# Attention and spectral mixing on one core: an earlier fold, a reordered end and equal output steps

## The chip, the core and the metric

The kernel runs on one core of a Trainium2 chip. Five engines work side by side, each through its own list of instructions in the order in which the program issued them: TensorE (PE, with its weight loads shown apart as PEld), VectorE (DVE), ScalarE (ACT), GpSimd (POOL) and SyncE (SP). POOL issues the transfers of the weights, SP those of the output. Engines wait for each other and for transfers through semaphores. The metric is the time of one execution in microseconds on the device; lower is better.

## The reference

First a causal attention with a forgetting gate, for 8 batches, 8 heads, 576 positions and 64 columns per head:

```python
scores = scale * np.matmul(q, k.transpose(0, 1, 3, 2))
cum = np.cumsum(np.log(np.clip(f, 0.0001, 1.0)), axis=-1)
scores = np.where(causal, -1e9, scores + cum[..., :, None] - cum[..., None, :])
attn = softmax(scores); x = np.matmul(attn, v)        # then heads side by side: (8, 576, 512)
```

Then a mixing in the frequency domain over the positions: the lowest 64 modes of x are multiplied, each by its own complex 512 x 512 matrix, brought back to positions and added, and a gated product ends it:

```python
X = np.fft.rfft(x, axis=1)
Yr = np.einsum('bmd,mde->bme', Xr, w_r) - np.einsum('bmd,mde->bme', Xi, w_i)
Yi = np.einsum('bmd,mde->bme', Xr, w_i) + np.einsum('bmd,mde->bme', Xi, w_r)
u = x + np.fft.irfft(Y, n=S, axis=1)
out = u + np.maximum(u @ w_ch, 0.0)
```

The weights w_r and w_i are 64 x 512 x 512 float32 each, 134 MB together, and are read once. The output is 9.44 MB of float32.

## The kernel before

There are three stages. The order on every engine is the order in which the source issues the work.

**Attention** runs over 32 pairs of heads and leaves x in `x_all` (128 positions per block; a batch has five blocks, the last with 64 positions only). Beside it the first weight tiles are loaded and multiplied.

**The weights' stage.** Modes are handled in groups of four, u = 0 to 15, and the 512 input columns in four quarters dc = 0 to 3. A weight tile (u, dc) has 1 MB in SBUF (2 MB in memory, cast to bfloat16 on the way). A pool of seven such buffers and POOL's transfers, issued one ahead of the next in the order of `wseq`, form a stream. For u < 15 `spec_mms` (L194) multiplies into an accumulator A; then `Yb` on DVE (L744) and four small products `yps` (L747) turn the result into mode columns: `YT` for the first 12 groups (96 rows of modes, real and imaginary), `YL` for the last four (32 rows). The last group, u = 15, is done with the weights as the stationary operand (`spec_cols`, L211: 32 products of 16 columns for one quarter), its sum over quarters being held in `accT`. The last tile (15,3) comes in four transfers, one for each mode.

In the gaps of this stage the PE does two other things for each batch. `xw(b)` computes x times w_ch into `XW[b]`. `fold(b)` adds the first 96 rows of modes, brought back to positions: `fold_modes` makes `y_sb` and `yw_sb` (the modes, and the modes times w_ch), then for each block three products and two copies put x + y back into `x_all` and XW + yw back into `XW`. Batches 0 to 5 are folded in u = 12 to 14, batch 6 in front of (15,1), batch 7 around (15,2).

**The output stage.** What is missing is the last 32 rows of modes. For a step the PE puts the *base* into PSUM (x_all or XW times an identity, L785) and adds the *rest* (32 rows of last modes times the inverse basis, L800) for two quantities, U and Z. ACT copies U (L854), DVE forms max(Z, 0) + U into `o_sb` (L855), and SP sends it (L860, L865). `last_modes(h)` makes the last modes for four batches: `pyl` turns them, `pywl` multiplies them by w_ch, and `yl` receives both.

The steps go over pairs of batches p and blocks sb: 16 steps of two 128-row tiles (512 KB), and 4 steps of one tile in which the two 64-row blocks of the pair lie one above the other (two transfers of 128 KB). The beginning of the stage in source order is

```python
first = bases(0)
AT = psU.tile([128, NEB, 8, B], F32, tag="u", name="AT2")
spec_cols(AT, NEB - 1)
...
last_modes(0)
for i, (p, sb) in enumerate(blocks):
    if i == 7:
        last_modes(1)
    U, Z = first if i == 0 else bases(i)
    rest(i, U, Z)
```

so the bases of step 0 are issued ahead of the products of the last weight tile. U and Z have four PSUM banks each (`psU`, `psZ`), taken over from the pools of the stage before.

Of the kernel before, what the change touches and what calls it, by code (L numbers as in the profile page):

```python
# [10 lines left out]
F32 = mybir.dt.float32  # L11
BF16 = mybir.dt.bfloat16
I32 = mybir.dt.int32
ALU = mybir.AluOpType
# [9 lines left out]
def kernel(  # L24
# [11 lines left out]
    nc = tc.nc  # L36
    B, H, S, Dh = q.shape
    NM = moe_w_r.shape[0]
    D = H * Dh
    assert S == 576 and Dh == 64 and D == 512 and H == 8, (B, H, S, Dh)  # L40
    assert NM == 64 and B == 8
    NSB = 5
# [5 lines left out]
    NF = 12  # L48
# [149 lines left out]
    def spec_cols(AT, dc):  # L198
        u = NU - 1
        w8 = wtile.pop((u, dc))  # L200
        for j in range(4):
            for eb in range(NEB):
                for n in range(2):
                    m = 4 * u + j
                    if dc < 2:
                        c0 = m * 24 + (8 if n == 0 else 0)
                        lhsT, rhs = w8[:, n, j, eb * 128 : (eb + 1) * 128], XS[:, dc, c0 : c0 + 16]
                    else:
                        c0 = 24 * n + (8 if dc == 2 else 0)
                        lhsT, rhs = w8[:, j, n, eb * 128 : (eb + 1) * 128], XPv[:, c0 : c0 + 16, m]  # L210
                    nc.tensor.matmul(  # L211
                        AT[:, eb, 2 * j : 2 * j + 2, :].rearrange("p c b -> p (c b)"),
                        lhsT=lhsT,
                        rhs=rhs,
                        start=(n == 0),
                        stop=(n == 1),
                    )
# [405 lines left out]
    with ExitStack() as bctx:  # L623
# [7 lines left out]

        with ExitStack() as mctx:
# [6 lines left out]
            def xw(b):  # L639

                xT = xtp.tile([128, NEB, S], BF16, tag="xT", name="xT")
                for eb in range(NEB):
                    ptr = psT.tile([128, S], BF16, tag="t", name="ptr")
                    for sc in range(NSB):
                        ns = SBLK[sc]
                        nc.tensor.transpose(
                            ptr[:, sc * 128 : sc * 128 + ns],
                            x_all[:ns, eb, b, sc, :],
                            ident_bf[:ns, :ns],
                        )  # L650
                    nc.vector.tensor_copy(xT[:, eb, :], ptr[:, :])  # L651
                if b < 3:
                    XW[b] = xw2.tile([128, NSB, D], BF16, tag="xw", name="XW")
                else:
                    XW[b] = yx[:, b - 3, :].bitcast(BF16).rearrange("p (s e) -> p s e", s=NSB)
                for sb in range(NSB):
                    Ms = SBLK[sb]
                    pxw = psX.tile([128, D], F32, tag="x", name="pxw")
                    for eb in range(NEB):
                        nc.tensor.matmul(  # L660
                            pxw[:Ms, :],
                            lhsT=xT[:, eb, sb * 128 : sb * 128 + Ms],
                            rhs=wch[:, eb, :],
                            start=(eb == 0),
                            stop=(eb == NEB - 1),
                        )
                    nc.scalar.copy(XW[b][:Ms, sb, :], pxw[:Ms, :])  # L667
# [27 lines left out]
            def fold(b, ys, sbs):  # L695

                y_sb, yw_sb = ys
                for sb in sbs:
                    Ms = SBLK[sb]
                    bi = BI[:KF, sb * 128 : sb * 128 + Ms]  # L700
                    pu = psX.tile([128, D], F32, tag="x", name="pu")
                    nc.tensor.matmul(
                        pu[:Ms, :], lhsT=ident_bf[:Ms, :Ms], rhs=x_all[:Ms, :, b, sb, :], start=True, stop=False
                    )
                    nc.tensor.matmul(pu[:Ms, :], lhsT=bi, rhs=y_sb[:KF, :], start=False, stop=True)  # L705
                    nc.scalar.copy(  # L706
                        x_all[:Ms, :, b, sb, :], pu[:Ms, :].rearrange("p (g c) -> p g c", g=NEB)
                    )
                    pz = psX.tile([128, D], F32, tag="x", name="pz")
                    nc.tensor.matmul(pz[:Ms, :], lhsT=bi, rhs=yw_sb[:KF, :], start=True, stop=True)  # L710
                    nc.vector.tensor_tensor(
                        XW[b][:Ms, sb, :], pz[:Ms, :], XW[b][:Ms, sb, :], ALU.add
                    )

            xw_plan = {2: 0, 3: 1, 5: 2, 6: 3, 7: 4, 8: 5, 9: 6, 10: 7}
            for u in range(NU):
# [4 lines left out]
                for dc in range(first, NEB - 1 if last else NEB):  # L721
                    if dc == NEB - 1 and u in xw_plan:
                        xw(xw_plan[u])
                    split = NSB
                    if u >= NF and dc < 3:
                        b = 2 * (u - NF) + dc - 1
                        split = 2 if b == B - 1 else NSB
                        ys = fold_modes(b)
                        fold(b, ys, range(split))
                    if last:  # L730
                        AT = psA.tile([128, NEB, 8, B], F32, tag="a", name="AT1")
                        spec_cols(AT, dc)
                        nc.vector.tensor_tensor(
                            accT[:], AT[:].rearrange("p e c b -> p e b c"), accT[:], ALU.add
                        )
# [3 lines left out]
                    if split < NSB:  # L739
                        fold(b, ys, range(split, NSB))  # L740
# [22 lines left out]
        usb = bctx.enter_context(tc.tile_pool(name="usb", bufs=4))  # L763
        psU = bctx.enter_context(tc.tile_pool(name="psU", bufs=4, space=PSUM))
        psZ = bctx.enter_context(tc.tile_pool(name="psZ", bufs=4, space=PSUM))
        blocks = [(p, sb) for p in range(B // 2) for sb in range(NSB)]
        yl = {}

        def parts(n):

            p, sb = blocks[n]
            Ms = SBLK[sb]
            if sb < NSB - 1:
                return [(2 * p + k, k, slice(0, Ms), sb, Ms) for k in range(2)]
            return [(2 * p + k, 0, slice(Ms * k, Ms * k + Ms), sb, Ms) for k in range(2)]

        def bases(n):

            pts = parts(n)
            nt = 1 + pts[1][1]  # L780
            U = [psU.tile([128, D], F32, tag="u", name="U") for _ in range(nt)]
            Z = [psZ.tile([128, D], F32, tag="z", name="Z") for _ in range(nt)]
            for which, ps in enumerate((U, Z)):
                for b, k, rows, sb, Ms in pts:
                    nc.tensor.matmul(  # L785
                        ps[k][rows, :],
                        lhsT=ident_bf[:Ms, :Ms],
                        rhs=XW[b][:Ms, sb, :] if which else x_all[:Ms, :, b, sb, :],
                        start=True,
                        stop=False,  # L790
                    )
            return U, Z

        def rest(n, U, Z):

            for which, ps in enumerate((U, Z)):
                for b, k, rows, sb, Ms in parts(n):
                    r = (b + 2 * which) % 4
                    grp = slice(32 * r, 32 * r + 32)
                    nc.tensor.matmul(  # L800
                        ps[k][rows, :],
                        lhsT=BI4[grp, sb * 128 : sb * 128 + Ms],
                        rhs=yl[b // 4][which][grp, :],
                        start=False,
                        stop=True,
                    )

        def last_modes(h):

            py = psU.tile([128, D], F32, tag="u", name="pyl")  # L810
            for eb in range(NEB):
                nc.tensor.matmul(
                    py[:, eb * 128 : (eb + 1) * 128],
                    lhsT=YL[:, eb, 4 * h : 4 * h + 4, :].rearrange("p b c -> p (b c)"),
# [5 lines left out]
            for eb in range(NEB):  # L820
                for n in range(2):
                    b = 4 * h + 2 * (1 - n)
                    nc.tensor.matmul(
                        pyw[64 * n : 64 * n + 64, :],
                        lhsT=YL[:, eb, b : b + 2, :].rearrange("p b c -> p (b c)"),
                        rhs=wch[:, eb, :],
                        start=(eb == 0),
                        stop=(eb == NEB - 1),
                    )
            yl[h] = [ylpool.tile([128, D], BF16, tag="yl", name="yl") for _ in range(2)]  # L830
            nc.scalar.copy(yl[h][0][:], py[:])
            nc.vector.tensor_copy(yl[h][1][:], pyw[:])

        first = bases(0)
        AT = psU.tile([128, NEB, 8, B], F32, tag="u", name="AT2")
        spec_cols(AT, NEB - 1)
        for h in range(2):
            bs = slice(4 * h, 4 * h + 4)
            nc.vector.tensor_tensor(
                YL[:, :, bs, KL - 8 : KL],  # L840
                AT[:, :, :, bs].rearrange("p e c b -> p e b c"),
                accT[:, :, bs, :],
                ALU.add,
            )
        last_modes(0)
        for i, (p, sb) in enumerate(blocks):
            if i == 7:
                last_modes(1)
            U, Z = first if i == 0 else bases(i)
            rest(i, U, Z)  # L850
            o_sb = wpool.tile([128, 2, D], F32, tag="w8", name="o_sb")
            for n in range(len(U)):
# [5 lines left out]
            s0 = sb * 128  # L858
            if len(U) == 2:
# [3 lines left out]
            else:  # L863
                for b, k, rows, _, Ms in parts(i):
                    nc.sync.dma_start(out[b, s0 : s0 + Ms, :], o_sb[rows, 0, :])  # L865
# [30 lines left out]
```

## Time and profile before

| what | value |
|---|---|
| median of 3 runs | 441.06 us (440.43 to 441.65) |
| the profiled execution | 442.7 us |
| its span, first to last instruction | 440.7 us |
| busy: PE, DVE, ACT, POOL | 344.5, 268.4, 233.3, 129.7 us |
| read from HBM, written | 163.73 MB, 9.44 MB |
| mean granted clock of the PE | 0.936 |
| last `AT` product issued from | 405.03 us |
| first output transfer issued | 410.50 us |
| last tile of `o_sb` done | 435.36 us |

Span and profiled execution differ by 2.0 us, which lie around the instructions. All times below are counted from the start of the span. Busy time says little on its own here, because the three stages have different limits; the chain of waits and the timeline of the last 60 us say what sets the end.

### The profile page before, as it was taken

Reading aid. Unit: us, or ns where it says so; the run is one execution under the profiler, and the core shown is the slowest. Engines: PE = TensorE matmul, PEld = TensorE weight load, DVE = VectorE, ACT = ScalarE, POOL = GpSimd, SP = SyncE. Lnnn points to the kernel's source line nnn. Section 1 sums busy time; section 2 is a strip of 40 time slices with the busy share of each in tenths; the row PEclk is TensorE's granted clock in tenths of the full one; section 3 lists DMA queues with packets and bytes.
Section 4 is the critical chain, followed back from the end, with each engine's and each line's share of the span. In section 5 each row is a group of like instructions: output and inputs, shape, how many; then the busy total and the mean of one; then the engine's idle time right before and its main releaser. Section 6 shows DMA issues by size and latency. Waiting matters only on the chain.

```text
span 440.7 us, 10287 instructions
## 1 busy us (share of the span) xinstructions
PE 344.5 (78%) x4295; PEld 189.9 (43%) x4305; DVE 268.4 (61%) x641; ACT 233.3 (53%) x355; POOL 129.7 (29%) x199
## 2 busy tenths in 40 slices
PE   1678878889889889898893694797885788979993
PEld 0455555555555565555551241343442233325331
DVE  6678888777887778888871221223231356635885
ACT  4567678778787665665640031132222355734673
POOL 6544444453454444444222111012211221100000
PEclk9999999999999999999997598599989699969997
DMA  8999999999999999999999999999999999992698
GB/s 190 205 234 221 230 220 231 232 228 227 231 231 222 231 222 229 221 230 224 232 212 212 212 212 212 212 212 212 211 212 210 211 210 210 210 210 53 219 347 294
DMA packets 68349, 96.75 MB, mean 220 GB/s; under 512 B 3536, under 2 KB 45008, under 8 KB 68304
## 3 DMA queue, kind: packets, MB, share of 16 engines
q0 software_dynamic: 62800, 85.64, 104.9%
q1 hardware_dynamic: 5504, 10.47, 6.8%
q8 instruction: 33, 0.54, 0.4%
q14 instruction: 12, 0.10, 0.1%
HBM read 163.73 MB, written 9.44 MB: 393 GB/s over the span
## 4 chain that ended last, share of the span: by engine, by line
DMA 39%; PE 34%; DVE 19%; ACT 3%; issue 3%; POOL 1%; DVEq 0%; POOLq 0%; ACTq 0%
DMA w<-in_moe_w_i_dram 22%; DMA w<-in_moe_w_r_dram 15%; DVE vT L384 5%; DVE x_all L492 4%; DVE qkT L360 4%; PE pav L477 4%; PE A L194 4%; PE sps L432 3%; PE tv L382 3%; PE pd L521 3%; PE vp L393 2%; PE U L785 2%; DMA qk<-in_k_dram 2%; PE Z L785 2%; DVE vn L372 2%
## 5 line engine op out<-in xcount | busy, mean ns | idle before, releaser
L439 ACT ACTIVATE et<-sps 128x1024 bf16<-128x1024 f32 x96 | 96.0, 1050 | 12.6 <-PE sps L432 10.2
L744 DVE TENSOR_TENSOR Yb<-A,yx 128x512 bf16<-128x512 f32 x15 | 10.4, 692 | 67.6 <-PE A L194 67.6
L477 PE MATMUL pav<-vs,et 128*128 128x65 bf16 (+1 forms) x896 | 51.2, 197 | 0.2 <-DVE vn L372 0.2
L360 DVE COPY qkT<-tp 128x640 bf16<-128x640 bf16 x64 | 48.8, 763 | 3.1 <-PE tp L355 3.0
L477 PEld LDWEIGHTS <-et 128*128 128x128 bf16 (+1 forms) x896 | 36.5, 102 | 17.2 <-issue 13.3
L194 PE MATMUL A<-w,XP 128*16 128x512 bf16 (+1 forms) x240 | 22.6, 457 | 27.1 <-DMA w<-in_moe_w_i_dram 15.6
L660 PE MATMUL pxw<-wch,xT 128*128 128x512 bf16 (+1 forms) x152 | 39.1, 403 | 1.0 <-DVE xT L651 0.4
L432 PE MATMUL sps<-qkT 64*128 64x512 bf16 (+4 forms) x320 | 38.9, 306 | 1.1 <-DVE qkT L360 1.1
L492 DVE TENSOR_TENSOR x_all<-pav,rcp 128x384 bf16<-128x384 f32 (+2 forms) x96 | 36.2, 377 | 3.3
L355 PE MATMUL tp<-ident_bf,qk 128*64 128x128 bf16 x576 | 29.3, 231 | 9.9 <-DMA qk<-in_k_dram 9.9
L384 DVE COPY vT<-tv 128x576 bf16<-128x576 bf16 x32 | 24.2, 757 | 19.3 <-PE tv L382 19.3
L667 ACT CAST XW<-pxw 128x512 bf16<-128x512 f32 (+1 forms) x15 | 8.8, 585 | 48.3 <-PE pxw L660 48.3
L165 POOL DMA_DIRECT2D w<-in_moe_w_r_dram x16 | 11.9, 743 | 70.1 <-PE A L194 56.7
L404 ACT COPY vs<-vp 128x576 bf16<-128x576 bf16 x32 | 20.5, 640 | 21.4 <-PE vp L400 21.4
L156 POOL DMA_DIRECT2D w<-in_moe_w_r_dram x27 | 20.5, 759 | 38.5 <-PE A L194 8.6
L667 ACT CAST yx<-pxw 128x512 bf16<-128x512 f32 (+1 forms) x25 | 14.6, 585 | 32.4 <-PE pxw L660 32.4
L165 POOL DMA_DIRECT2D w<-in_moe_w_i_dram x19 | 13.3, 700 | 55.8 <-PE A L194 26.1
L109 POOL DMA_DIRECT2D qk<-in_q_dram x32 | 19.7, 614 | 33.8 <-PE tp L355 7.8
L706 ACT CAST x_all<-pu 128x512 bf16<-128x512 f32 (+1 forms) x40 | 23.4, 584 | 9.0 <-PE pu L705 8.0
L491 DVE RECIPROCAL rcp<-pav 128x6 f32<-128x6 f32 (+2 forms) x96 | 16.2, 169 | 16.3 <-PE pav L477 16.1
L156 POOL DMA_DIRECT2D w<-in_moe_w_i_dram x27 | 20.4, 756 | 17.5 <-DMA w<-in_moe_w_i_dram 8.2
L109 POOL DMA_DIRECT2D qk<-in_k_dram x32 | 19.4, 605 | 20.2 <-DMA w<-in_moe_w_r_dram 6.5
(134 smaller groups left out, 666.5 us busy)
## 6 DMA issues: line engine op xcount, KB each, us to landing
w<-in_moe_w_r_dram POOLq DMA_DIRECT2D x16, 1024.0 KB, 29.6
w<-in_moe_w_i_dram POOLq DMA_DIRECT2D x15, 1024.0 KB, 32.1
w<-in_moe_w_r_dram POOLq DMA_DIRECT2D x27, 512.0 KB, 11.1
w<-in_moe_w_i_dram POOLq DMA_DIRECT2D x27, 512.0 KB, 12.5
vt<-in_v_dram POOLq DMA_DIRECT2D x29, 288.0 KB, 10.6
out_dram<-o_sb SPq DMA_DIRECT2D x16, 512.0 KB, 3.4
qk<-in_q_dram POOLq DMA_DIRECT2D x32, 144.0 KB, 10.7
qk<-in_k_dram POOLq DMA_DIRECT2D x32, 144.0 KB, 10.8
```

Of the source, the lines that this page charges most:

```text
L109: nc.gpsimd.dma_start(qk[64 * n : 64 * n + 64, :, :], src[b, 2 * g : 2 * g + 2, :, :].rearrange("h (p r) d -> p h (r d)", p=64),)
L156: nc.gpsimd.dma_start(w8[:, t, :, :], src[4 * u : 4 * u + 4, dc * 128 : (dc + 1) * 128, :].rearrange("m p e -> p m e"),)
L165: nc.gpsimd.dma_start(w8[:, j : j + step, :, :].rearrange("p m r e -> p m (r e)"), src[m : m + step, 256:512, :].rearrange("m (p r) e -> p ...
L194: nc.tensor.matmul(A[32 * j : 32 * j + M, :], lhsT=lhsT, rhs=rhs, start=st_, stop=sp_)
L355: nc.tensor.transpose(tp[64 * hp : 64 * hp + 64, r - r0, :, :].rearrange("p n c -> p (n c)"), qk[:, hp, r * 64 : r * 64 + 64], ident_bf[:, :],
L360: nc.vector.tensor_copy(st[i]["T"][:].rearrange("p n (c r) -> p n c r", r=9)[:, :, :, r0:r1], tp[:, 0 : r1 - r0, :, :].rearrange("p r n c ...
L384: nc.vector.tensor_copy(st[i]["vT"][:].rearrange("p (c r) -> p c r", r=9), tv[:].rearrange("p r c -> p c r"))
L432: nc.tensor.matmul(ps[:, hp, c : c + n], lhsT=KT[sl, jb * 128 : jb * 128 + 128], rhs=QT[sl, i0 : i0 + n], start=True, stop=True,)
L439: nc.scalar.activation(st[i]["et"][:, T, :, :], ps[:], ACT.Exp, scale=scale)
L477: nc.tensor.matmul(pav[:Ms, sb % 3, hp, :], lhsT=eblk(i, hp, jb, sb), rhs=rhs, start=(jb == 0), stop=(jb == sb),)
L492: nc.vector.tensor_tensor(x_all[:ns, g, b, lo:hi, :].rearrange("p s (h d) -> p s h d", h=2), pav[:ns, lo % 3 : lo % 3 + n, :, 0:Dh], _stri ...
L660: nc.tensor.matmul(pxw[:Ms, :], lhsT=xT[:, eb, sb * 128 : sb * 128 + Ms], rhs=wch[:, eb, :], start=(eb == 0), stop=(eb == NEB - 1),)
```

## The change

Five edits, all behind the last of the u = 14 products of quarter 2, apart from one that only moves data:

1. The 64-row blocks of an odd batch are kept in rows 64 to 127 of the even batch's tile (`place`), in `x_all` and in `XW`, from `xw` and `fold` on.
2. Folding is laid out by a table `before`: batch 6's modes and first two blocks stand ahead of the products of (14,3), its other blocks ahead of (15,1); batch 7's modes and two blocks stand ahead of (15,2); its other three blocks each ahead of one mode of (15,3).
3. (15,3) is multiplied inside the weights' loop, mode by mode, and so ahead of the output's bases.
4. In `last_modes`, `pywl` is four products with 128 columns of weights in place of eight with 64. Its halves come out in the other order and are copied crosswise: DVE copies 64 rows, and ACT the other 64 rows after the first step's copies.
5. The output has 18 steps of two tiles: 16 as before, and 2 that join the 64-row blocks of two pairs of batches (as steps 7 and 16). A base of such a tile is one full product. Steps 0, 1 and 17 send each tile by itself. Output transfers: 24 before, 23 now.

```diff
+        def place(b, sb):
+            if sb < NSB - 1:
+                return slice(0, 128), b
+            return slice(64 * (b % 2), 64 * (b % 2) + 64), b - b % 2
...
-                    nc.scalar.copy(XW[b][:Ms, sb, :], pxw[:Ms, :])
+                    nc.scalar.copy(XW[to][rows, sb, :], pxw[rows, :])
...
+            for b in range(6):
+                before[(NF + b // 2, 1 + b % 2)] = [(b, range(NSB))]
+            before[(NU - 2, 3)] = [(6, range(0, 2))]
+            before[(NU - 1, 1)] = [(6, range(2, NSB))]
+            before[(NU - 1, 2)] = [(7, range(0, 2))]
...
+            def folds(work):
+                for b, sbs in work:
+                    if b not in ys:
+                        ys[b] = fold_modes(b)
+                    fold(b, ys[b], sbs)
...
+                    folds(before.get((u, dc), []))
                     if last:
                         AT = psA.tile([128, NEB, 8, B], F32, tag="a", name="AT1")
+                        if dc < NEB - 1:
+                            spec_cols(AT, dc)
...
+                        else:
+                            for j in range(4):
+                                if j < 3:
+                                    folds([(7, [2 + j])])
+                                spec_cols(AT, dc, [j])
...
-        blocks = [(p, sb) for p in range(B // 2) for sb in range(NSB)]
+        last64 = NSB - 1
+        steps = [[(p, sb), (p, sb)] for p in range(B // 2) for sb in range(last64)]
+        steps.insert(15, [(2, last64), (3, last64)])
+        steps.insert(7, [(0, last64), (1, last64)])
...
             for eb in range(NEB):
-                for n in range(2):
-                    b = 4 * h + 2 * (1 - n)
-                    nc.tensor.matmul(
-                        pyw[64 * n : 64 * n + 64, :],
-                        lhsT=YL[:, eb, b : b + 2, :].rearrange("p b c -> p (b c)"),
-                        rhs=wch[:, eb, :],
...
+                nc.tensor.matmul(
+                    pyw[:], lhsT=cols[eb], rhs=wch[:, eb, :], start=(eb == 0), stop=(eb == NEB - 1)
+                )
...
-            nc.vector.tensor_copy(yl[h][1][:], pyw[:])
-
-        first = bases(0)
-        AT = psU.tile([128, NEB, 8, B], F32, tag="u", name="AT2")
-        spec_cols(AT, NEB - 1)
...
+            nc.vector.tensor_copy(yl[h][1][64:128, :], pyw[0:64, :])
+            return lambda: nc.scalar.copy(yl[h][1][0:64, :], pyw[64:128, :])
+
+        second = last_modes(0)
+        for i in range(len(steps)):
             if i == 7:
-                last_modes(1)
-            U, Z = first if i == 0 else bases(i)
-            rest(i, U, Z)
+                second = last_modes(1)
+            U = base(i, 0)
+            if i == 0:
+                rest(i, 0, U)
+                Z = base(i, 1)
+            else:
+                Z = base(i, 1)
+                rest(i, 0, U)
+            rest(i, 1, Z)
...
+            alone = i in (0, 1, len(steps) - 1)
...
+                if n == 1 and second is not None:
+                    second()
+                    second = None
+                if alone:
+                    nc.sync.dma_start(out[2 * p + n, s0 : s0 + 128, :], o_sb[:, n, :])
+            if sb == last64:
+                for j in range(2):
+                    nc.sync.dma_start(
+                        out[2 * p + j : 2 * p + j + 3 : 2, s0:S, :].rearrange("b p e -> p b e"),
+                        o_sb[64 * j : 64 * j + 64, :, :],
+                    )
```

## The prediction, made before the changed kernel ran

> **What bounds the kernel now.** I read the page's slices and its chain first, then the chain piece by piece from 359 us on, the timeline and one-microsecond stretches there, and last the landing of single transfers. Up to 387.8 us the bound is the weights' stream: one piece of the chain is a wait of 28.41 us for a transfer, after which the PE stays on the path almost without a gap.
>
> ```profile
> 359.39 28.41 DMA w<-in_moe_w_i_dram
> 387.84 1.09 PE A L194 x7
> 388.95 0.70 DVE Yb L744
> ...
> 397.77 0.26 PE py L673 x4
> ...
> 400.65 0.91 PE AT L211 x32
> 401.56 0.22 PE pu L702
> ...
> 405.03 1.09 PE AT L211 x32
> 406.14 0.30 DVE YL L839
> 406.49 0.41 PE pyl L812 x4
> ```
>
> These are start, length and work. The last products of all (third `AT` row) start at 405.03. When did their weights land? Their four transfers of 256 KB were issued at 373.36, 375.63, 378.25 and 383.18 and took 25.7, 24.7, 23.4 and 19.7 us: landings at 399.06, 400.33, 401.65 and 402.88. In the same way tile (15,1) is complete at 363.26 + 29.7 = 392.96 and (15,2) at 368.44 + 29.4 = 397.84. So at the end the PE runs 2.1 us behind the stream. Why behind?
>
> ```profile
> w<-in_moe_w_i_dram POOLq DMA_DIRECT2D x1, 256.0 KB, 19.7
> ```
> ```profile
> 385.00:386.00 1.00, 0.91 (x10) 0.30 (x9) 0.81 (x2) 0.58 (x1) 0.00 (x0) 1.00 1.19 206
> 386.00:387.00 1.00, 0.00 (x0) 0.00 (x0) 0.12 (x1) 0.00 (x0) 0.00 (x0) 1.00 1.22 207
> 387.00:388.00 1.00, 0.16 (x4) 0.16 (x7) 0.00 (x0) 0.00 (x0) 0.00 (x0) 0.80 1.21 210
> 388.00:389.00 1.00, 0.90 (x8) 0.00 (x2) 0.05 (x1) 0.00 (x0) 0.00 (x0) 0.50 1.18 205
> ```
>
> Columns: stretch, length, busy time of PE, PEld, DVE, ACT, POOL, granted clock, DMA share, GB/s. The PE idles 1.93 us (385.91 to 387.84) waiting for weights, and from 387.5 to 394.5 its clock is 0.5: batch 6 is folded at half speed (`pu` 0.43 us instead of 0.22).
>
> The third stage is the output loop, where PE, DVE and writes are nearly equal:
>
> ```profile
> 429.21 0.59 PE L785 MATMUL Z<-yx,ident_bf 128*128 128x512 bf16 x2
> 429.49 5.87 DVE L855 SCALAR_TENSOR_TENSOR o_sb<-Z,u_sb 128x512 f32<-128x512 f32 x9 [0.30 <-ACT u_sb L854]
> 435.39 1.99 SPq L865 DMA_DIRECT2D out_dram<-o_sb  x2
> ```
>
> A DVE tile takes 5.87/9 = 0.652 us, a step of two tiles 1.30; the PE's starts of such steps lie 1.29 to 1.40 apart (mean 1.315), those of a 64-row step 0.88. The last tile ends at 435.36, 5.34 us before the end of the span.
>
> **The change, part by part.**
>
> *Folding moved up.* No folding work is added. Batch 6's modes and two blocks go ahead of A(14,3), into the idle patch. The same work for batch 7 took 397.77 to 400.65 = 2.88 us at full clock, with a wait for `yw_sb` inside. So 385.91 + 2.88 = 388.79; A(14,3), 0.65 us at full clock (385.26), ends 389.44, its weights there since 387.84. Queued behind is Yb, which now also stands behind two XW additions on DVE: batch 7's second one ended 3.68 us after its start, so here 389.59; Yb 0.70 and yps 0.39 bring 390.73. That delay is covered, since YL is wanted only after 403. Three blocks of batch 6 (401.56 to 403.74 = 2.18) reach 392.9; AT(15,1) waits for 392.96, +0.91 = 393.9; batch 7's modes and two blocks +2.88 = 396.8; AT(15,2) waits for 397.84, ends 398.75. Then block, four-mode part and so on: 0.65 + 0.25 twice gives 400.55 (parts landed at 399.06 and 400.33), the 64-row block 0.88 gives 401.43, part three waits for 401.65 and ends 401.92, part four waits for 402.88 and ends **403.2**. Before: 406.12. Gain 2.9, all that the stream allows; the two waits (1.0 us each) are also the cover, so the front can be 1 us slower per piece without cost. POOL's weight issues end at 383.18 and are not passed.
>
> *Last products ahead of the bases; `pywl` with four.* Before, bases(0) stood ahead of AT(15,3) and their Z waited for a PSUM slot (404.59). Now pyl starts 0.37 after AT as before, 403.57, ends 403.90. pywl: eight 64-column products took 0.98; four full ones by batch 7's pyw (0.88) end 404.78. U's base 0.54, U's rest 0.32, Z's base 0.53, Z's rest 0.32: step 1 starts at 406.5 instead of 409.1. The bases are back on the path, but half covered by the DVE copy of yl (0.69), so 0.3 of the 2.9 are given back: **2.6**. ACT's second half copy (a 64-row cast: 0.58, L706) stands behind step 0's copies and is needed only by step 4; in step 7 it adds 0.59 to an ACT that idled 1.05 there: nothing, or +0.35 if that idle time is gone.
>
> *Joined 64-row blocks.* Before, steps 1 to 19 took the PE 15 x 1.315 + 4 x 0.88 + 1.31 (last_modes) = 24.56 (409.1 to 433.64: 24.5). The joined step has four full bases (0.87) and eight rest products of 32 rows; four such took 0.33 together (413.57). Bounds: eight together 0.33, one after another 8 x 0.22 = 1.76. Nearest is the four-wide row, as only four row groups exist in the operands: two rounds, 0.55, with 0.10 for the change of form 1.52. Now 15 x 1.315 + 2 x 1.52 + 1.21 = 23.98: **0.55** saved (0.95 saved to 1.9 lost by the bounds), PE end 430.5. DVE still has 36 tiles. From Z's rest to the end of two tiles takes 2.33 us (410.01 to 412.34), so last tile at 432.5 (before 435.36).
>
> *Last step in two single transfers.* Before, after the last tile, two 128 KB transfers left at 435.39 and 435.98 and took 3.8 and 3.7; the span ended 1.0 after the second's landing. Now the last 256 KB leave at 432.5. Bounds: 2.6 (a 512 KB one's 3.2 less 0.65 of its own data) to 3.8; I take 3.4. Plus 1.0: end at 436.9. Steps 0 and 1 also go as halves: two more issues on SP of 0.37 us each, hidden under 1.3 us steps; the first leaves 0.65 earlier.
>
> Moving XW's and x_all's odd 64-row blocks to rows 64 to 127 changes no instruction's shape: nothing (the 64-row casts cost 0.58, as the full ones do).
>
> Sum: 440.7 - 436.9 = **3.8 us off**. The profiled execution took 442.7 (2.0 around its span), so 438.9 for one like it; the median of the runs shown is 441.06, so 437.3.
>
> **The rivals.**
>
> *The clock falls again, in the new waits.* The granted clock changes on a grid of about 3.4 us (387.5 down, 394.5 up, 319.4 down, 322.8 up). It fell where the PE had been busy 0.56, 0.45 or 0.25 of the 3.4 us before, not at 0.61 (308 to 310). My schedule idles 0.22 + 0.96 + 0.37 us between 401.4 and 403.6: 0.55 if a window holds it all, which depends on where the grid lies. Price: one window at half speed just as the output starts, 3.4/2 = 1.7 us: 439.0. For it: the share; against: three windows in four hold less of it. The Trainium skill (TensorE: Matmul & The Clock Gate, HAM oscillation) asks only for no PE-idle gaps over about 3.4 us, by which the clock would stay up. The trace differs: 1.93 us were enough at 387.5.
>
> *Slower: half speed that lasts.* Same place, but the clock stays at 0.5 for three windows, as in 237.4 to 254.6 or 339.8 to 350.2. Each window costs 1.7; from three on (5.1) it is 442.4 and slower. Against: those stretches had a PE waiting for weights; windows of 0.94 and 1.0 busy (322.6, 394.4) brought the clock back, and this loop is that full.
>
> *The writes become the bound.* Eighteen equal steps ask 512 KB per 1.31 us = 400 GB/s; the page's second-last slice shows 347. At 347, 9.44 MB take 27.2 us; from 408.2 (first issue 407.4 + 0.8) to 435.4, with 1.8 until landing and 1.0 after it 438.2, so 438.6 by the median. Against: transfers issued 1.30 apart from 424.63 to 428.62 landed after a steady 3.2 to 3.3 us, no queue growing. The Trainium skill (DMA: Bandwidth & Descriptors, Specifications) states about 358 GB/s per core at HBM; slices of 1.55 us at 391 and 395 GB/s here exceed it.
>
> *It doesn't do what it says:* if folding batch 6 early also delays what follows by over 2 us, only the loop's and the end's 1.2 us remain: 439.9. Both covers of 1 us speak against it.
>
> **How the numbers follow.** Forecast 0.55; clock falls once 0.24; writes bound 0.11; front not gained 0.06; lasting half speed 0.04. 437.3 is the likeliest; the range 435.6 to 439.7 takes the joined step's and the end's good bounds (0.4 + 0.8, with some spread of runs) below, the clock and the writes above, and leaves out the last two. About 0.3% (1.3 us, so 439.7 and 442.4) is what can be told from no change: faster 0.90, same 0.06, slower 0.04.
>
> **What would show it.** PE busy between 386 and 388 and the clock 1.0 at 388 to 394; the last `AT` product near 403.2, directly after a weight's landing; the first output transfer near 407.4; 17 step starts 1.31 apart and joined ones at 1.5; the end 4.4 us after the last tile. It is wrong if the last `AT` comes past 404.5, if the clock is 0.5 after 403, or if the transfers' landing grows step by step above 4.3 us.

## The result, and the profile after

The changed kernel takes 443.76 us (median of 10 runs, 442.03 to 446.26) against 441.12 us (440.00 to 443.26): 1.0057 of the time before, 95% interval [1.0032, 1.0082]. It is slower by 2.6 us where 3.8 us less were forecast, and the range of 435.6 to 439.7 doesn't hold it. The profiled execution took 445.22 us, 1.5 more than the median, its span 443.2 us. A run over 1.5% above the fastest of its kernel counts as slow and is left out of the ratios, which among all the runs here concerns three of e1_fold_only alone.

The chain of waits of the changed kernel, in order of time (start, length, work):

```profile
397.13 1.08 PE AT L211 x32
...
399.16 0.43 PE pu L710
...
403.05 0.30 DVE YL L761
...
404.01 1.71 PE pywl L856 x4
405.71 0.85 PE U L818 x2
...
408.61 0.97 PE U L818 x2
...
412.95 0.54 PE U L818 x2
```

The front did what was forecast: the first YL addition starts at 403.05 where it started at 406.14, and the forecast had the last product end at 403.2. Part of that match is luck: the last weights landed at 402.10 here, 0.8 us earlier than in the profile before, and the last product ended 0.69 us behind them, where 0.3 was forecast. But look at the lengths. A block's `pu` takes 0.43 at 399.16, four `pywl` products take 1.71 (0.88 was counted), and U's two bases 0.85 to 0.97, until at 412.95 the same work takes 0.54 again. One-microsecond stretches of the same kernel (columns as in the prediction; the third number from the end is the granted clock) say why:

```profile
397.00:398.00 1.00, 0.87 (x31) 0.88 (x32) 0.00 (x0) 0.00 (x0) 0.00 (x0) 1.00 0.76 137
398.00:399.00 1.00, 1.00 (x20) 0.61 (x16) 0.42 (x1) 0.32 (x1) 0.00 (x0) 0.83 0.68 127
408.00:409.00 1.00, 1.00 (x5) 0.28 (x5) 0.29 (x1) 0.80 (x2) 0.00 (x0) 0.50 0.00 0
412.00:413.00 1.00, 1.00 (x7) 0.21 (x6) 0.91 (x2) 0.10 (x2) 0.00 (x0) 0.85 0.00 0
```

The clock fell at 398.7, after the wait for (15,2) (1.11 us idle before 397.13), and came back at 412.3: 13.7 us at half speed, four steps of the clock's 3.4 us grid, with the first steps of the output inside. Step 3, the fourth, starts at 412.88; by the forecast (step 1 at 406.5, then 1.31 us per step) it would have been 409.1.

Two smaller things stand further on. DVE's timeline has two gaps around step 7 (the bracket is the idle time before):

```profile
421.38 1.29 DVE L883 SCALAR_TENSOR_TENSOR o_sb<-Z,u_sb 128x512 f32<-128x512 f32 x2 [0.40 <-ACT u_sb L882]
423.52 2.53 DVE L883 SCALAR_TENSOR_TENSOR o_sb<-Z,u_sb 128x512 f32<-128x512 f32 x4 [0.86 <-ACT u_sb L882]
```

And the end is longer. SP's timeline:

```profile
435.62 1.27 SPq L893 DMA_DIRECT2D out_dram<-o_sb  x2
436.99 2.35 SPq L890 DMA_DIRECT2D out_dram<-o_sb  x2
```

Issuing a transfer takes SP 0.37 us in the loop, but here 0.6 to 1.2, so that the last tile, done at 437.10, leaves only at 438.1. From the last tile to the end it takes 6.1 us; 4.4 were forecast, 5.34 was it in the first profile before (5.9 and 5.6 in b1 and b2 below). The stretches of the same kernel at the end show the transfer engines busy throughout (second number from the end), but moving less than before:

```profile
434.00:436.00 2.00, 1.17 (x8) 0.30 (x6) 1.66 (x4) 1.57 (x4) 0.00 (x0) 1.00 1.04 381
438.00:440.00 2.00, 0.00 (x0) 0.00 (x0) 0.00 (x0) 0.00 (x0) 0.00 (x0) 0.90 0.99 258
```

Of the 6.3 us between forecast span (436.9) and measured span, 4.6 lie before the last tile (437.1 against 432.5) and 1.7 behind it. This adds up within one execution, and a long one; whether the forecast's starting point was right is another question, which the experiments had to ask too.

### The profile page after: what moved, and what is told of

Same layout as the page of the kernel before. It is cut to its first block, busy times and chain, and to the rows that moved or that the text cites. A ratio compares the mean times of both kernels' runs of the same rounds, so it can differ in the third digit from the quotient of the medians.

```text
span 443.2 us, 10268 instructions
## 1 busy us (share of the span) xinstructions
PE 352.6 (80%) x4289; PEld 191.5 (43%) x4289; DVE 268.7 (61%) x641; ACT 234.4 (53%) x357; POOL 129.2 (29%) x199
## 4 chain that ended last, share of the span: by engine, by line
PE 43%; DMA 30%; DVE 19%; ACT 3%; issue 2%; POOL 1%; DVEq 0%; POOLq 0%; ACTq 0%
DMA w<-in_moe_w_r_dram 14%; DMA w<-in_moe_w_i_dram 12%; PE pav L477 5%; PE A L194 5%; DVE vT L384 5%; DVE qkT L360 4%; DVE x_all L492 4%; PE pxw L667 4%; PE sps L432 4%; PE pd L521 3%; PE tv L382 3%; PE vp L393 3%; PE U L818 2%; PE Z L818 2%; DMA qk<-in_q_dram 2%
## 5 line engine op out<-in xcount | busy, mean ns | idle before, releaser
L477 PE MATMUL pav<-vs,et 128*128 128x65 bf16 (+1 forms) x896 | 52.7, 200 | 0.2 <-DVE vn L372 0.2
L477 PEld LDWEIGHTS <-et 128*128 128x128 bf16 (+1 forms) x896 | 37.7, 104 | 18.2 <-issue 13.7
L432 PE MATMUL sps<-qkT 64*128 64x512 bf16 (+4 forms) x320 | 40.3, 315 | 1.1 <-DVE qkT L360 1.1
L667 PE MATMUL pxw<-wch,xT 128*128 128x512 bf16 (+1 forms) x160 | 40.7, 410 | 0.0
L355 PE MATMUL tp<-ident_bf,qk 128*64 128x128 bf16 x576 | 30.3, 237 | 9.0 <-DMA qk<-in_k_dram 9.0
L156 POOL DMA_DIRECT2D w<-in_moe_w_r_dram x27 | 20.4, 757 | 38.0 <-PE A L194 7.7
L883 DVE SCALAR_TENSOR_TENSOR o_sb<-Z,u_sb 128x512 f32<-128x512 f32 x36 | 23.2, 686 | 6.8 <-ACT u_sb L882 3.9
```

The lines of the kernel that those rows point to most:

```text
L156: nc.gpsimd.dma_start(w8[:, t, :, :], src[4 * u : 4 * u + 4, dc * 128 : (dc + 1) * 128, :].rearrange("m p e -> p m e"),)
L355: nc.tensor.transpose(tp[64 * hp : 64 * hp + 64, r - r0, :, :].rearrange("p n c -> p (n c)"), qk[:, hp, r * 64 : r * 64 + 64], ident_bf[:, :],
L432: nc.tensor.matmul(ps[:, hp, c : c + n], lhsT=KT[sl, jb * 128 : jb * 128 + 128], rhs=QT[sl, i0 : i0 + n], start=True, stop=True,)
L477: nc.tensor.matmul(pav[:Ms, sb % 3, hp, :], lhsT=eblk(i, hp, jb, sb), rhs=rhs, start=(jb == 0), stop=(jb == sb),)
L667: nc.tensor.matmul(pxw[rows, :], lhsT=xT[:, eb, sb * 128 : sb * 128 + Ms], rhs=wch[:, eb, :], start=(eb == 0), stop=(eb == NEB - 1),)
```

## The experiments

All are compared with runs of the kernel before on the same chip. Three theories: the clock's fall lost the time; the edits of the output stage lost it; the gain was never there to be had.

**e1_fold_only.** The kernel before with only the fold moved up.

```diff
+                    if (u, dc) == (NU - 2, NEB - 1):
+                        ys6 = fold_modes(6)
+                        fold(6, ys6, range(2))
+                    if (u, dc) == (NU - 1, 1):
+                        fold(6, ys6, range(2, NSB))
```

> The kernel before with one edit: batch 6's modes and first two blocks ahead of the products of (14,3), its other blocks ahead of (15,1); bases of step 0 stay ahead of the last products, output steps as before. Clock theory (the time was lost to half speed at the start of the output, set off by the new waits): the last AT ends near 403.2 instead of 406.1, the bases fill the wait for the last weights, the clock stays at 1.0 from 388 on, span about 437.8, 2.9 us under before (ratio 0.993). If the clock still falls after the remaining 1.1 us wait for (15,2), it falls near 398 and the gain shrinks to 0 to 1.5 us. Rival (the loss comes from the edits of the output stage, not from the clock): also about 2.9 us under before, whatever the clock does.

Measured: 441.70 us against 441.64; without its three longest runs (445.85 to 446.89) the median is 440.58 and the ratio 0.9985 [0.9959, 1.0011]. The profiled execution kept its clock and had a span of 438.6. But the runs spread widely, 438.9 to 446.9. No gain can be shown.

**e2_fill.** The changed kernel with products into an unread PSUM tile in its two waits; nothing else differs.

```diff
+        def fill(pool, tag, k):
+            junk = pool.tile([128, D], F32, tag=tag, name="junk")
+            for _ in range(k):
+                nc.tensor.matmul(junk[:], lhsT=ident_bf[:], rhs=wch[:, 0, :], start=True, stop=True)
...
+                        if dc == 2:
+                            fill(psT, "t", 5)
...
+                                else:
+                                    fill(psT, "t", 4)
```

> The changed kernel with idle-time products that nobody reads: five 128x512 products ahead of (15,2), four ahead of the last mode of (15,3), 0.22 us each, in the two waits for weights. Clock theory: the clock stays at 1.0 from 398 to 413, step 3 of the output starts near 409.5 instead of 412.9, the time falls by 3 to 4 us against the changed kernel, to about 440 (ratio to before 0.996 to 0.999). Rival (the output edits lose the time): the time stays at the changed kernel's 443.8 (ratio 1.006) although the clock is up.

Measured: 441.55 us, ratio 1.0004 [0.9984, 1.0024]: 2.2 us under the changed kernel although it does more work (e3 and e4 below, measured beside it and with the waits left empty, take 443.45 and 443.93). The stretches of this kernel where the clock was down before:

```profile
398.00:399.00 1.00, 0.94 (x5) 0.48 (x5) 0.97 (x2) 0.59 (x1) 0.00 (x0) 1.00 0.63 123
408.00:409.00 1.00, 0.85 (x7) 0.10 (x4) 0.91 (x2) 0.38 (x1) 0.00 (x0) 1.00 0.00 0
```

The clock theory holds, but the 2.2 us are a third of the 6.5 between forecast (437.3) and measured, and 440 wasn't reached: something else is missing.

**e3_last_whole** and **e4_pywl_eight**, each the changed kernel with one thing undone: the split of the last step, and the crosswise `yl` with its copy on ACT.

```diff
-            alone = i in (0, 1, len(steps) - 1)
+            alone = i in (0, 1)
```
```diff
-                nc.tensor.matmul(
-                    pyw[:], lhsT=cols[eb], rhs=wch[:, eb, :], start=(eb == 0), stop=(eb == NEB - 1)
-                )
+                for n in range(2):
+                    b = 4 * h + 2 * (1 - n)
+                    nc.tensor.matmul(
+                        pyw[64 * n : 64 * n + 64, :],
+                        lhsT=YL[:, eb, b : b + 2, :].rearrange("p b c -> p (b c)"),
+                        rhs=wch[:, eb, :], start=(eb == 0), stop=(eb == NEB - 1),
+                    )
...
-            nc.vector.tensor_copy(yl[h][1][64:128, :], pyw[0:64, :])
-            return lambda: nc.scalar.copy(yl[h][1][0:64, :], pyw[64:128, :])
+            nc.vector.tensor_copy(yl[h][1][:], pyw[:])
```

> The changed kernel with the last step sent as one 512 KB transfer after both tiles. Theory that the last small transfers queue on SP (the last tile was done at 437.1, its transfer issued at 438.0 and landed 4.4 later): one issue fewer, the transfer leaves 0.03 after the tile and lands 3.6 to 4.1 later, end 0.5 to 1.0 us earlier than the changed kernel's 6.1 after the last tile. Rival (writes are behind anyway and splitting helps, as the change has it): 0 to 0.7 us later.

> The changed kernel with w_ch on the last modes in eight products of 64 columns again, one DVE copy of 128 rows, and no second copy on ACT. If the second ACT copy causes the stall between steps 7 and 9 (DVE idle 0.40 and 0.86, one PE step 1.88 instead of 1.31): that PE step takes 1.3 to 1.4 and the time falls by 0.4 to 0.6 us against the changed kernel. Rival (the stall comes from last_modes as before, 0.72 idle there): no difference, or 0.1 to 0.2 us more for the eight products.

Measured: 443.45 us, 1.0042 [1.0025, 1.0060], and 443.93 us, 1.0050 [1.0024, 1.0076]. In both profiles the clock fell as in the changed kernel (398.1 to 408.4 and 397.6 to 407.8: three steps of the grid). Splitting the last step neither costs nor gains what can be told: e3 needs 6.2 us from the last tile to the end, where 0.5 to 1.0 less than 6.1 were expected. In e4's timeline the gap of 0.86 falls to 0.22, as one theory said, while the one ahead of step 7 grows from 0.40 to 0.74:

```profile
420.08 1.29 DVE L888 SCALAR_TENSOR_TENSOR o_sb<-Z,u_sb 128x512 f32<-128x512 f32 x2 [0.74 <-ACT u_sb L887]
421.59 12.07 DVE L888 SCALAR_TENSOR_TENSOR o_sb<-Z,u_sb 128x512 f32<-128x512 f32 x18 [0.22 <-ACT u_sb L887]
```

Yet the time doesn't fall. Compared with e3, whose clock was down as long, e4 has its last tile 0.5 us earlier (435.2 and 435.7), and both spans are 441.9. The last 512 KB transfer ahead of the second joined step, issued at 432.29, needs 5.8 us to land in e4, its like in the changed kernel 3.8. DVE's tiles came earlier and then waited longer in the queue of the writes. First line e4, second fence the changed kernel (views of the transfers; size, median us from issue to landing):

```profile
out_dram<-o_sb SPq DMA_DIRECT2D x1, 512.0 KB, 5.8
```
```profile
out_dram<-o_sb SPq DMA_DIRECT2D x1, 512.0 KB, 3.8
```

**e5_fold_fill**: e1 with five filler products ahead of (15,2). **e8_fold_fill_end**: e5 with the output order of the last pair changed.

```diff
+                        if dc == 2:
+                            fill(5)
...
-        blocks = [(p, sb) for p in range(B // 2) for sb in range(NSB)]
+        blocks = [(p, sb) for p in range(B // 2 - 1) for sb in range(NSB)]
+        blocks += [(B // 2 - 1, sb) for sb in (0, 4, 1, 2, 3)]
```

(the second part in e8 only)

> The kernel before with batch 6's fold moved up as in e1_fold_only, and five products that nobody reads in the 1.1 us wait for (15,2). e1's profile kept the clock at 1.0 and had a span of 438.6, but its runs lay between 438.9 and 446.9. Clock theory: the long ones are those where the clock fell in that wait; filled, they go, all runs lie between 438.5 and 441.5, median about 439.3 (ratio 0.993 to 0.997). Rival (the spread has another cause): spread and median as e1's, 441.7.

> As e5_fold_fill, with the 64-row step of the last pair of batches second in its pair, so that the output ends with a 512 KB step. If 64-row transfers at the end cost (5.3 to 5.7 between last tile and end): 0.3 to 0.8 under e5_fold_fill. Rival (the last tile is then a two-tile step, 0.65 later): no difference.

Measured: 440.46 us, 0.9988 [0.9969, 1.0007], and 440.74 us, 0.9986 [0.9967, 1.0006], before 441.47. e5's runs lie between 439.6 and 443.0: the long runs of e1 are gone, as the clock theory said, though no profile caught one of them. But the medians lie 1.0 us apart, not 2.2, and the interval of the ratio includes 1. The order at the end makes no difference that can be told.

**e6_joined_early** and **e7_joined_four**, both e2_fill with one more edit:

```diff
-        steps.insert(15, [(2, last64), (3, last64)])
+        steps.insert(10, [(2, last64), (3, last64)])
```
```diff
-                for j in range(2):
-                    nc.sync.dma_start(
-                        out[2 * p + j : 2 * p + j + 3 : 2, s0:S, :].rearrange("b p e -> p b e"),
-                        o_sb[64 * j : 64 * j + 64, :, :],
-                    )
+                for b, k, rows, _, Ms in parts(i):
+                    nc.sync.dma_start(out[b, s0:S, :], o_sb[rows, k, :])
```

> The changed kernel with the filler products of e2_fill, and the second joined step as step 11 in place of 16. Theory that transfers of joined steps move slowly (after 436 the DMA engines of the changed kernel are busy 0.96 to 1.06 at only 219 to 309 GB/s, where 512 KB transfers run at 380 to 390): at the end only the last two 256 KB transfers are left of this, the end comes 5.3 or less after the last tile instead of 6.0, the time falls 0.5 to 1.0 under e2_fill's 441.6. Rival (the end is one of total bytes at the engines' rate, wherever the joined step stands): no difference.

> The changed kernel with the filler products of e2_fill, and each joined step sent as four transfers of 128 KB, one for each batch, as the kernel before sends its 64-row blocks. If the pattern of two batches in one 64-row transfer is what moves slowly: 0.5 to 1.0 under e2_fill, and 350 GB/s or more in the two microseconds behind such a step. If 64 rows in themselves move slowly (64 of 128 partitions): no difference or up to 0.5 more, from two issues more on SP.

Measured: 441.43 us, 1.0003 [0.9986, 1.0019], and 440.35 us, 0.9990 [0.9972, 1.0007]. Moving the joined step doesn't help: in e6 it stands in the middle (issued at 425.1), and the loss moves with it, as two-microsecond stretches show:

```profile
424.00:426.00 2.00, 2.00 (x15) 0.62 (x14) 1.78 (x4) 1.34 (x4) 0.00 (x0) 1.00 1.04 388
426.00:428.00 2.00, 2.00 (x12) 0.61 (x10) 1.89 (x4) 1.68 (x4) 0.00 (x0) 1.00 1.02 267
428.00:430.00 2.00, 2.00 (x15) 0.55 (x14) 1.99 (x4) 1.52 (x3) 0.00 (x0) 1.00 1.00 293
430.00:432.00 2.00, 1.33 (x12) 0.37 (x8) 1.89 (x4) 1.72 (x4) 0.00 (x0) 1.00 1.05 401
```

The transfer engines are busy throughout, at two thirds to three quarters of their rate for 4 us. e7's median is 1.1 us lower, though its rate behind a joined step did not reach the 350 GB/s expected (335 and 301 at the end). Behind the first joined step it is as low as e6's, and in the profile of the kernel before, too, the rate falls while the 64-row transfers issued at 423.04 and 423.57 move. First e6, then e7, then two stretches of the kernel before:

```profile
420.00:422.00 2.00, 2.00 (x15) 0.62 (x15) 2.00 (x4) 1.46 (x4) 0.00 (x0) 1.00 0.85 197
```
```profile
420.00:422.00 2.00, 2.00 (x14) 0.62 (x14) 2.00 (x4) 1.46 (x4) 0.00 (x0) 1.00 0.92 197
```
```profile
424.00:426.00 2.00, 2.00 (x12) 0.61 (x11) 1.89 (x4) 1.68 (x4) 0.00 (x0) 1.00 0.98 313
426.00:428.00 2.00, 2.00 (x17) 0.74 (x16) 1.99 (x4) 1.78 (x4) 0.00 (x0) 1.00 1.05 396
```

So the rate goes with the 64 rows, not with two batches in one transfer, as e7's rival had it, though that rival gave no gain in time. Four transfers differ in another way: two of them need only the first tile of the step. In e7 the first left at 418.47, 0.03 us after the first tile, in e6 at 418.95, 0.02 after the second; the first tiles were done at 418.44 and 418.33.

**b1_before_look, b2_before_look**: the kernel before, unchanged. **b3_before_fill**: the kernel before with eight filler products ahead of (14,3), `fill(8)`. **e9_mended**: e7 and e4 together.

> The kernel before itself, for another profile. The prediction took the front's gain (2.9 us) from one profiled execution, 1.6 us longer than the median. Theory that this execution had a clock fall at 387.5 that the median one lacks: here, if the run is near 441 or under, the clock stays at 1.0 from 386 to 395 and the first YL addition starts 1.0 to 2.0 us earlier than 406.14, counted from the same distance to the last weight's landing (3.2 us behind it in the profiled one). Rival (the fall belongs to every execution): clock 0.5 behind the wait again and YL 3 us behind the landing.

> As b1_before_look, a second look at the kernel before, with the same expectations; two looks, since the clock's grid lies differently in each execution.

> The kernel before with eight products that nobody reads (1.76 us) in the wait ahead of (14,3). If the clock's fall in that wait costs every execution: about 1.5 us under before (ratio 0.996 to 0.998). If the median execution doesn't have it: no difference (0.999 to 1.001) and a narrower spread.

> The changed kernel with the filler of e2_fill, joined steps sent as four transfers, and w_ch on last modes in eight products with one DVE copy. By the parts' prices (filler -2.2, four transfers -1.1, second copy -0.4 from the changed kernel's 443.8): 440.0, ratio 0.995 to 0.998. Rival (the writes set the end and swallow the last 0.4): as e7_joined_four, 440.4.

b1 took 441.26 us and b2 440.92 us. In both the clock stayed at 1.0 from 379 us on until the PE had finished. b1's chain and stretches (line numbers are one higher there):

```profile
388.11 0.67 PE A L195 x8
...
392.04 0.22 PE pu L703
...
404.14 0.30 DVE YL L840
```
```profile
387.00:388.00 1.00, 0.00 (x0) 0.00 (x0) 0.00 (x0) 0.00 (x0) 0.00 (x0) 1.00 1.21 209
388.00:389.00 1.00, 0.65 (x8) 0.17 (x7) 0.20 (x1) 0.00 (x0) 0.00 (x0) 1.00 1.19 208
```

The wait ahead of (14,3) is the same as in the first profile (1.95 us), but the clock doesn't fall in it, `pu` takes 0.22, and YL starts at 404.14. In b1 the last product ends 0.93 us behind the landing of its weights, in the first profile 3.2. b1 and b2 lie nearer to the medians of the kernel before (441.1 to 442.2) than the 442.7 of the first profile; how many of its runs have the fall isn't recorded. b3 gave 441.17 us, 0.9987 [0.9969, 1.0005], no difference that can be told, as expected if the median execution doesn't have the fall, though its spread is no narrower. e9 gave 441.36 us, 0.9998 [0.9978, 1.0018]: neither the 440.0 expected nor the rival's 440.4, and by its ratio not to be told from e7.

**e10 to e13, measured side by side**, because medians taken at different times didn't settle what joined transfers cost. e10 is e5, e11 is e2_fill and e12 is e7, each with `fill(6)` ahead of the products of (13,3) as well; e13 is the changed kernel itself.

> As e5_fold_fill, with six more products that nobody reads (1.3 us) in the wait ahead of (13,3), where the clock fell at 372 in two of the profiles of this front (e2_fill, b3_before_fill) and in b2_before_look. Theory that this earlier fall, where it happens, leaves the PE behind the stream up to YL (22 us from the last weight's issue in e2_fill and 22.9 in b3_before_fill, against 20.2 to 20.7 without a fall): 0.3 to 0.8 under e5_fold_fill's 440.5, all runs under 442, ratio 0.995 to 0.998. Rival (a fall at 372 is made up before the end): as e5_fold_fill.

> The changed kernel with the filler of e2_fill and six more products ahead of (13,3): joined steps go out as two transfers of 256 KB, two batches each. With the clock held, what is left of the loss is the output stage: YL to end 36.1 to 36.3 as in e2_fill and e6_joined_early, time 440.9 to 441.5.

> As e11_pairs_fill_two, but joined steps go out as four transfers of 128 KB. If two batches in one 64-row transfer cost 1.0 us (YL to end 36.2 against 35.2 in e7_joined_four and 35.3 in e9_mended): 1.0 under e11_pairs_fill_two in the same call, 440.0 to 440.5. Rival (those distances differ by chance, as the medians of e6, e7 and e9 don't follow them): within 0.4 of e11_pairs_fill_two.

> The changed kernel itself beside the two above, on the same chip, for the clock's price within one call and a further look at whether it falls near 398. Clock theory: it falls again, 442 to 446, 2 to 2.5 us over e11_pairs_fill_two. Rival: it stays up in about half of the executions, seen as runs at 441.

| kernel | median us (runs) | ratio to before, 95% interval |
|---|---|---|
| before | 442.17 (440.4 to 444.0) | 1 |
| e13, the changed kernel | 444.11 (441.0 to 445.8) | 1.0040 [1.0017, 1.0062] |
| e11, clock held | 441.85 (440.9 to 442.7) | 0.9990 [0.9975, 1.0004] |
| e12, clock held, four transfers | 440.33 (439.3 to 441.7) | 0.9957 [0.9940, 0.9973] |
| e10, only the fold moved, clock held | 440.55 (439.5 to 441.2) | 0.9962 [0.9943, 0.9981] |

So side by side the clock costs the changed kernel 2.3 us, and two transfers for a joined step in place of four another 1.5. e10 and e12 are faster than the kernel before beyond their intervals, and by every comparison than the changed one. e10 and e12 lie within 0.2 us of each other: the edits of the output stage, in their best form here, add nothing that can be told to the moved fold. e10 can't be told from e5 (440.55 and 440.46), and e11 is a little above the 441.5 expected. e13's clock fell again, at 399.6, for 13.7 us.

The profiles side by side; the first distance runs from the issue of the last weight transfer to the first YL addition (it takes out how early the stream ended in each execution), the second from there to the end of the span:

| profile | issue to YL | YL to end | clock at 0.5 between 360 us and the last tile |
|---|---|---|---|
| before, the one predicted from | 22.96 | 34.6 | 387.6 to 394.4 |
| b1, b2 | 20.69, 20.70 | 35.1, 34.8 | none; 375.1 to 378.5 |
| changed, e13 | 20.66, 20.61 | 40.2, 40.2 | 398.7 to 412.3; 399.6 to 413.2 |
| e3, e4 | 21.24, 21.26 | 38.2, 38.2 | 398.1 to 408.4; 397.6 to 407.8 |
| e2 | 21.91 | 36.3 | 372.3 to 379.1 |
| e6, e11 | 20.19, 20.20 | 36.1, 36.4 | none |
| e7, e9, e12 | 20.2 in all | 35.2, 35.2, 36.0 | none |
| e1, e5, e8, e10 | 20.4 to 20.6 | 34.9, 34.8, 35.0, 35.1 | none |
| b3 | 22.86 | 34.9 | 372.3 to 379.1 |

## Why the prediction was wrong, point by point

*Folding moved up: 2.9 us forecast, 0 to 0.5 there by the profiles.* This is the first failed step. Its schedule came close: counted from the last weight's issue the last product was to end after 20.0 us, and the YL addition starts after 20.7, or 20.2 with the clock held. What it was compared with was wrong: YL at 406.14 in the profiled execution, whose clock had fallen in its own wait. In b1 and b2 the kernel before reaches YL 20.7 us behind the last weight's issue. The sign was there to be read: the profiled execution took 442.7, 1.6 more than the median, and the forecast subtracted the whole gain from the median as well, as if each run had that 1.6 us in it. In the medians e10, the moved fold with unread products in two waits, is 1.6 us under before. That is more than the distances show; that the rest is what the unread products spare it of falls of the clock is likely, but not shown.

*The clock, forecast to stay at 1.0 (0.55 against 0.24 and 0.04).* This is the second failed step. Near 398 the clock fell in all four profiles with this front and unfilled waits (the changed kernel, e3, e4, e13), and in none of the six with both waits filled (e2, e6, e7, e9, e11, e12), nor in the three of e1's front with its one wait filled; e1's own profile kept it too. The rival looked at the waits from 401.4 to 403.6. The fall came ahead of them, behind the wait for (15,2), which the forecast's schedule also has (396.8 to 397.84). The rival's shares would not have told it: the prediction has falls at 0.56 (0.51 by its rows, for the fall at 387.6) and less, and here the PE had been busy 0.67 of the 3.4 us before. The length, 10 to 14 us, was that of the rival given 0.04. "This loop is that full" is the argument that failed: the PE was busy without a break from 403.4 on, and the clock came back at 412.3. The price of 1.7 us per step of the grid was too high. From the last weight's issue to the end it takes 56.3 and 56.6 us where the clock never fell after 360 us (e6, e11), 59.5 with three steps (e3, e4) and 60.8 with four: 1.0 to 1.1 a step. In the medians the clock costs 2.2 (e2) and 2.3 (e11); the two profiles with four steps are runs of 445.2 and 445.8 us, above the medians of 443.8 and 444.1.

The Trainium skill (TensorE: Matmul & The Clock Gate, What's actually happening) says that the clock comes back after at least one busy window of about 3.4 us and is lost after at least one idle one. The trace agrees with the 3.4 us grid. It differs on the fall, which came with no gap over 1.11 us and the PE busy 0.67 of the 3.4 us before; and one busy window was not enough for the return, as the clock stayed at 0.5 until 412.3, where the PE had been busy without a break since 403.4.

*Joined blocks: 0.55 saved forecast, nothing saved.* The PE's price was right (the joined steps start 1.51 and 1.62 before the next, forecast 1.52). But the PE isn't what ends there. From the first tile's start to the last tile's end it takes 26.17 in b1, 26.95 in e11, and 26.23 in e9, which joins the blocks but copies `yl` on DVE alone. DVE has 36 tiles in all three, so that joining saves nothing, and the crosswise copy costs 0.7: that copy had been forecast at nothing or 0.35, by the idle time ACT had in step 7.

*The end: 1.0 saved forecast, nothing saved.* This step, too, was mis-sized. From the last tile to the end it takes 6.1 us in the changed kernel, 5.34 in the first profile and 5.9 and 5.6 in b1 and b2. Against the 4.4 forecast, the last 256 KB leave 1.0 us after their tile, not at once, land after 3.9, not 3.4, and 1.2 follow, not 1.0. The step took the landing of a 512 KB transfer less its own half and left out what stands ahead of it: transfers of 64 rows that run at 258 to 293 GB/s with the engines busy 0.99 to 1.02, and hold up SP. The Trainium skill (DMA: Bandwidth & Descriptors, Rules for kernel authors) advises against two transfers to disjoint partition halves and for one of 128 partitions. The kernels before and after both do the former with their 64-row blocks, and in both the trace shows rate lost there (313 GB/s before and 267 in e6, in the stretches above). Four transfers for a joined step are 1.5 us faster than two (e11, e12), at a like rate. Of this, some 0.6 can be the earlier start of the first two, which need not wait for the second tile; no run separates the two.

*The writes become the bound (0.11)* was half right. Tiles that come earlier mostly wait longer to land (e4 against e3; e9 against e7, where the last tile comes 0.5 us sooner after the YL addition, and the end 0.1 later), so gains inside the loop hardly reach the end; the rate is lost in the 64-row transfers, while the plain ones nearly keep 400 GB/s.

Together, from the runs taken side by side: +1.9 us for the changed kernel, of which +2.3 the clock, +1.5 two transfers in place of four, and -1.8 the rest, which e10 shows to be the front with its waits filled (-1.6) almost alone.

Still open: what exactly the clock's gate counts, since shares of busy time do not predict it; and what besides the earlier start makes four transfers better than two (e12's distance from YL to the end, 36.0, is hardly under e11's 36.4, while the medians differ by 1.5).

## What to carry to other kernels

Set a saving against the execution that the median stands for: where the profiled one is longer, find what made it longer first, and take a second profile, since a clock that fell there gives a gain that other runs don't have. Idle time that a change moves is not gone: ask where it comes to lie, and whether the work behind it can afford half speed; two microseconds of unread products, put into two waits, were worth 2.2. And when a loop's engines and its writes are nearly equal, as here, taking work off one of them gains little, while transfers that move slowly cost at any place.

## What the runs showed of the hardware

The clock came back only after 10 to 14 us in the output's first steps, with the PE busy 0.8 of each 3.4 us or more, while batch 6's fold in the first profile had it back after 7. The same 1.9 us wait ahead of (14,3) brought it down in one profile and not in another (the stretches of b1 above). SP's issue of a transfer, 0.37 us for most steps of the loop, takes 0.6 to 1.2 us for the last ones of the changed kernel, which follow each other closely. Writes of 512 KB steps run at 381 to 401 GB/s in the stretches shown; where 64-row transfers move, the rate is 197 to 313, with the transfer engines 0.85 to 1.02 busy.
